# Key-tile sums moved to VectorE in six of twelve head pairs, with loads, reciprocals and key layout rearranged, in a fused attention and gated-MLP kernel

## The chip, the cores and the metric

One core of one Trainium2 chip runs the whole program. The metric is device time in microseconds (us) of one execution. Before the change three runs gave a median of 324.01 us (323.78 to 324.86).

## The reference

```python
# attention, B, H, S, D = 2, 12, 448, 64
scores = cap * np.tanh((q @ k^T) / sqrt(D) / cap)
attn = np.exp(scores - max(scores)) 
attn = attn / (sum(attn) + 1e-9)
x = (attn @ v) laid out as (B, S, H * D)
# gated MLP with a spatial gate: x is 768 wide, d_ff 1024
u, v = split(gelu(x @ w_in))
x = x + (u * (w_sg @ layernorm(v) + b_sg)) @ w_out
# second MLP: depthwise convolution of width 3 along the sequence
h = relu(x @ w2_in);  out = (h * sigmoid(conv(h))) @ w2_out
```

The inputs are scaled so that the cap is active. All of it is float32.

## The kernel before

The 24 heads are worked as 12 **pairs** N = 0 to 11, two heads in the two halves of the 128 partitions. Each pair has two half-steps, R = 2N and R = 2N + 1, in the loop at line 609, which also issues loads and calls `tick` twice per half-step; `later(k, fn)` runs `fn` k ticks on. TensorE (PE) executes one written order: `ordered` pins each product behind the one before.

- `scores` (line 386) makes the transposed scores, keys in the partitions. The even half makes key tiles 0 and 1 from split operands Q and K (12 products), the odd half tile 2 and the 64 keys that are left (8 products from raw qr and kr). Both write one PSUM tile `sc` with a single buffer, so the next half's products wait until ScalarE's tanh (line 397) has read it. ScalarE then applies exp (line 406). VectorE adds tiles 0 and 1 of the even half into `sm` (line 462).
- `values` (line 490) runs two half-steps behind: products of the exponentials with V (`V`, `vlast`), then the softmax sums as products with a tile of ones: four of `sm` after the even half, four of tile 2 and four of the rest after the odd half. Output and sums stand in PSUM `pv`.
- `norm` (line 516): ScalarE copies `pv` to `E` (line 532). For two pairs at once, POOL-issued DMAs gather the sums into `ss`; VectorE adds a guard and inverts (lines 552, 553); DMAs spread the reciprocals over DRAM `d` into `rb`; VectorE multiplies (line 569) and splits the result into X (`part`).
- `decode` turns the weights, which arrive as 64-bit floats, into split float32. One **piece** of `w_in` is a DMA into `f`, then a cast of the head (line 155 on VectorE, 153 on ScalarE), a shift-and-or (159), a cast (165) and a subtraction (168). `WIN` says at which half-step each of the 12 pieces is issued.
- After half-steps 15, 19, 23 and at the end, products of the first MLP stand among the attention's (`FILL`); from about 100 us on PE works the two MLPs.

The order of instructions on VectorE, ScalarE, POOL and SyncE's DMA queue comes from a scheduler that sorts by its own timing model, bounded by data and by `pin`, which puts an instruction behind an earlier one on its engine. These queues are strictly in order. I call the stretch from the first score product of pair N to that of pair N + 1 **window N**; PE does there scores of N and values of N - 1.

Of the kernel before, what the change touches and what calls it, by code (L numbers as in the profile page):

```python
# [16 lines left out]
ALU = mybir.AluOpType  # L17
# [20 lines left out]

TAKEN = 4

WARM = 10

K0 = 2 * P

IDLE = {0: (1, 4)}

WIN = (3, 5, 7, 9, 12, 15, 17, 19, 21, 22, 23, 24)
WOS = (0, 0, 1, 4, 4, 7, 7, 7, 10, 10, 11, 15)
W2I = (12, 12, 13, 13, 15, 17, 22, 24, 26, 30, 30, 33)
W2O = (0, 0, 1, 3, 4, 6, 7, 8, 8, 10, 10, 11, 11, 11, 11, 12, 13, 14, 15, 17, 18, 18, 19, 19)  # L50
# [3 lines left out]
def stages(  # L54
# [19 lines left out]

    now = [0]
    guards = [None]
    lasta, lastv, lastr, lasts = [None], [None], [None], [None]

    def pin(last):
        return tc.issue_after(last[0].ins) if last[0] is not None else ExitStack()  # L80
# [54 lines left out]
    heads = []  # L135
    drain = [None]

    def decode_half(hi, lo, src, pool, bufs, wait, hi_eng, top_eng, cols):

        n = src.shape[1]  # L140
        r = pool.tile([P, cols, 2], U32, tag="f64", name="f64", bufs=bufs)[:, :n]
        words = r.rearrange("p c w -> p (c w)").bitcast(U16)
        sync(words[:, : 4 * n - 1], src.rearrange("r c w -> r (c w)").bitcast(U16)[:, 1:])
        low = r[:, :, 0]
        top = words.rearrange("p (c w) -> p c w", w=4)[:, :, 2].bitcast(BF16)
        heads.append(heads.pop(0))
        hd = heads[-1][:, :n]

        def s1():
            half = hd.bitcast(F16).rearrange("p (c w) -> p c w", w=2)[:, :, 1]  # L150
            with pin(lasta), pin(lastv):
                if top_eng == "a":
                    A.activation(half, top, AF.Copy)  # L153
# [19 lines left out]
    def decode(hi, lo, src, pool, bufs, wait=(1, 2, 3), hi_eng="a", cols=512, low_eng="v", top_eng="a"):  # L173

        if heads:
            return decode_half(hi, lo, src, pool, bufs, wait, hi_eng, top_eng, cols)
        n = src.shape[1]
        r = pool.tile([P, cols, 2], U32, tag="f64", name="f64", bufs=bufs)[:, :n]
# [99 lines left out]

    def columns(pool):
        sync(gbc, g_ln.partition_broadcast(P))  # L280
        decode(cw[:, 0], cw[:, 1], conv_w, pool, *((4, (5, 6, 7)) if bounded else (3,)))

    def attention(att, psa):

# [6 lines left out]

        def load(n):
            b, p = divmod(n, NPAIR)
            qr = att.tile([P, S], F32, tag="qr", name="qr", bufs=3)
            kr = att.tile([P, S], F32, tag="kr", name="kr", bufs=3)
            k0 = 0 if n else K0
            for h in range(2):
                r = slice(h * D, (h + 1) * D)
                dma = sync if n or h else nc.scalar.dma_start
                dma(qr[r], qT[b, p, r, h])  # L300
                if k0:
                    dma(kr[r, :k0], kT[b, p, r, h, D * h : D * h + k0])

            sync(kr[:D, k0:], kT[b, p, :D, 0, k0:])
            sync(kr[D:, k0:ST], kT[b, p, D:, 1, D + k0 :])
            sync(kr[D:, ST:], kT[b, p, D:, 1, :D])
# [20 lines left out]
        def prep_k(n):  # L327
            _, kr = qraw[n]
            K = Kt[n % 2]
            lastv[0] = split(kr[:, :K0], K[:, 0], K[:, 1])  # L330

        G.dma_start(capt, cap.partition_broadcast(P))
        load(0)
# [2 lines left out]
        vlast = att.tile([P, B * NPAIR, P], F32, name="vlast")  # L336

        def load_vlast(n0, n1):
            v = vL.rearrange("b n p g c -> p (b n) g c")
            for h in range(2):  # L340
                r = slice(h * D, (h + 1) * D)
                for c in range(2):
                    sync(vlast[c * D : (c + 1) * D, n0:n1, r], v[r, n0:n1, 3, r])

        load_vlast(0, 3)
# [40 lines left out]
        def scores(N, half, then=None):  # L386
# [28 lines left out]
            for g in range(2 * half, 2 * half + 2):  # L415
# [10 lines left out]
                elif g == 2:  # L426
                    qr, kr = qraw[N]
                    x = qr.rearrange("p (i c) -> p i c", i=2)
                    for h in range(2):
                        r = slice(h * D, (h + 1) * D)  # L430
                        for i in range(2):
                            o, w = slice(i * D, (i + 1) * D), slice(K0 + i * D, K0 + (i + 1) * D)
                            ordered(ps[o, h, :2], lhsT=kr[r, w], rhs=x[r], start=True, stop=True)
                else:

                    qr, kr = qraw.pop(N)
                    for h in range(2):
                        r = slice(h * D, (h + 1) * D)
                        for i in range(2):
                            ordered(  # L440
                                ps[i * D : (i + 1) * D, h, 2], lhsT=kr[r, ST:],
                                rhs=qr[r, i * HS : (i + 1) * HS], start=True, stop=True,
                            )
                if N == 0 and g < 2:
# [45 lines left out]
        def values(N, half, done=False):  # L490
# [8 lines left out]
            ps, su, both = acc[N]  # L499
            raw = raws.pop((N, half))  # L500

            for g in range(2 * half, 3 * half + 1):
                x = raw if half else held.pop(N)
                for t in range(4):
                    h, c = divmod(t, 2)
                    ordered(
                        su[t * 32 : (t + 1) * 32],
                        lhsT=ones[2 if g < 3 else c],
                        rhs=x[:, h, g - 2 + c if g == 2 else 2] if half else x[:, h, c * HS : (c + 1) * HS],
                        start=False, stop=g == 3, tile_position=(0, t * 32), skip_group_check=True,  # L510
                    )
            if half:
# [3 lines left out]
        def norm(N, both):  # L516
# [31 lines left out]


            def s1():  # L550
                with pin(lastv):
                    V.tensor_scalar(out=ss, in0=ss, scalar1=guard, scalar2=None, op0=ALU.add)
                V.reciprocal(out=ss, in_=ss)
                ds.append(dr.tile([m, 2, 2, HS], F32, tag=f"d{m}", name="d"))
# [10 lines left out]
                        )  # L565

            def s2():
                with pin(lastv):
                    V.tensor_tensor(out=eb, in0=eb, in1=rb, op=ALU.mult)
                part(0)  # L570

            def part(i):
                with pin(lasta) if N >= 8 else pin(lastv):
                    lastv[0] = split(eb[:, i], X[:, 0, p - j + i, b], X[:, 1, p - j + i, b], "a" if N >= 8 else "v")

            k = 5 if N < 8 else 4
# [32 lines left out]
        for R in range(2 * NN + LAGS[1] + 1):  # L609
# [2 lines left out]
                columns(att)  # L612
            for j, at in enumerate(WIN):
                if at == R:
                    top_eng = "v" if R < 11 else "a"
                    wdec(*wi_piece(w_in, j // NK, j % NK), att, 4, hi_eng="v", wait=(5, 6, 7), top_eng=top_eng)
            if R < 2 * NN:
                if half == 0 and N + 2 < NN:
                    load(N + 2)
                if half == 0 and N + 1 < NN:  # L620
                    load_v(N + 1)
                if R == 6:
                    load_vlast(3, NN)
# [50 lines left out]
            tick()  # L674
        assert not due
        heads.clear()
        lasta[0] = lastv[0] = None
        lasts.clear()

    def exact_attention(att, psa):  # L680
# [420 lines left out]
```

## Time and profile before

| | |
|---|---|
| Median of 3 runs | 324.01 us |
| Profiled execution: time, span | 323.47 us, 321.3 us |
| Granted TensorE clock, mean | 0.997 |
| Busy: PE, VectorE, ScalarE, POOL | 313.5, 222.0, 206.6, 37.4 us |

The profiled execution is 0.54 us faster than the median, and 2.2 us of its time lie around the span. A matmul's record ends later than the next one starts, since they are pipelined, so durations on PE are read from start to start. Busy shares average over stages: VectorE and ScalarE are nearly idle in the last fifth.

### The profile page before, as it was taken

How to read it: one execution, taken by the hardware profiler on the slowest of the kernel's cores; microseconds unless marked ns; L12 is line 12 of the kernel's file. 1: busy time of each engine (PE TensorE's matmuls, PEld its weight loads, DVE VectorE, ACT ScalarE, POOL GpSimd, SP SyncE). 2: the span in 40 equal slices, each digit the busy share in tenths (PEclk: the TensorE clock that was granted, in tenths of full speed). 3: DMA queues.
4: the chain of work that ended last, by engine and by line, in shares of the span. 5: the costliest groups of instructions: out<-in, count | busy, mean ns of one | idle time of the engine just before them, and what ended most of it. 6: DMA issues, size and time to landing. Idle time of an engine off the chain costs nothing.

```text
span 321.3 us, 6377 instructions
## 1 busy us (share of the span) xinstructions
PE 313.5 (98%) x2398; PEld 259.3 (81%) x2398; DVE 222.0 (69%) x460; ACT 206.6 (64%) x342; POOL 37.4 (12%) x75
## 2 busy tenths in 40 slices
PE   8999999999999999999999999999999999999993
PEld 6566656666677889988999999999999999999992
DVE  3458596698568879988996899979999998000000
ACT  4999989898973447746944754568886988111010
POOL 3000141441333020211112000000000000000000
PEclk9999999999999999999999999999999999999998
DMA  3478886857242153331134670021583201110111
GB/s 114 116 219 209 246 232 151 240 165 243 93 131 89 31 159 97 93 98 50 51 98 134 203 285 1 3 65 66 141 317 98 74 27 58 58 60 29 57 57 39
DMA packets 24528, 37.73 MB, mean 117 GB/s; under 512 B 7609, under 2 KB 22473, under 8 KB 24489
## 3 DMA queue, kind: packets, MB, share of 16 engines
q1 hardware_dynamic: 22552, 34.22, 35.1%
q0 software_dynamic: 1632, 2.61, 2.8%
q8 instruction: 21, 0.34, 0.5%
q10 hardware_dynamic: 304, 0.41, 0.4%
q14 instruction: 19, 0.15, 0.2%
HBM read 34.39 MB, written 2.79 MB: 116 GB/s over the span
## 4 chain that ended last, share of the span: by engine, by line
PE 81%; DMA 2%; DVE 0%; ACT 0%; SPq 0%; issue 0%; ACTq 0%
PE mo L113 18%; PE mo L112 18%; PE mo L114 18%; PE pv L380 8%; PE sc L380 4%; PE mo L795 3%; PE mo L797 3%; PE mo L796 3%; PE mo L380 3%; PE fi L380 2%; DMA ss<-E 1%; DMA kr<-in_kT_dram 1%; PE mo L841 1%; PE mo L842 1%; DVE sm L462 0%; ACT o L982 0%
## 5 line engine op out<-in xcount | busy, mean ns | idle before, releaser
L113 PE MATMUL mo<-X,WI 128*128 128x448 f32 x120 | 43.9, 366 | 0.0
L114 PE MATMUL mo<-X,WI 128*128 128x448 f32 x120 | 43.8, 365 | 0.0
L112 PE MATMUL mo<-X,WI 128*128 128x448 f32 x120 | 43.4, 365 | 0.0
L406 ACT ACTIVATE raw<-raw 128x1344 f32<-128x1344 f32 (+2 forms) x25 | 36.4, 1460 | 0.7
L397 ACT ACTIVATE raw<-sc 128x1792 f32<-128x1792 f32 (+1 forms) x22 | 32.4, 1474 | 4.4 <-PE sc L380 4.4
L112 PE MATMUL mo<-HG,W 128*128 128x448 f32 x96 | 34.4, 365 | 0.0
L114 PE MATMUL mo<-HG,W 128*128 128x448 f32 x96 | 34.4, 365 | 0.0
L113 PE MATMUL mo<-HG,W 128*128 128x448 f32 x96 | 34.4, 365 | 0.0
L380 PE MATMUL pv<-raw,V 128*32 128x224 f32 x576 | 32.9, 357 | 0.0
L985 ACT ACTIVATE o<-mo 128x448 f32<-128x448 f32 x11 | 5.8, 540 | 34.9 <-PE mo L114 31.7
L380 PEld LDWEIGHTS pv<-raw,V 128*32 128x32 f32 x576 | 19.0, 109 | 11.5 <-issue 5.6
L113 PEld LDWEIGHTS mo<-X,WI 128*128 128x128 f32 x120 | 22.5, 188 | 1.9
L114 PEld LDWEIGHTS mo<-X,WI 128*128 128x128 f32 x120 | 22.5, 188 | 1.9
L112 PEld LDWEIGHTS mo<-X,WI 128*128 128x128 f32 x120 | 22.5, 188 | 1.9
L153 ACT ACTIVATE hs<-f 128x256 f16<-128x256 bf16 x36 | 16.6, 488 | 7.8 <-DMA f<-in_w_in_dram 4.8
L114 PEld LDWEIGHTS mo<-HG,W 128*128 128x128 f32 x96 | 18.0, 188 | 1.4
L113 PEld LDWEIGHTS mo<-HG,W 128*128 128x128 f32 x96 | 18.0, 188 | 1.4
L112 PEld LDWEIGHTS mo<-HG,W 128*128 128x128 f32 x96 | 18.0, 188 | 1.4
L168 DVE TENSOR_TENSOR WI<-f,WI 128x256 fp32r<-128x256 f32 (+1 forms) x36 | 18.2, 509 | 1.0 <-ACT WI L163 0.7
L113 PE MATMUL mo<-gl,WO 128*128 128x448 f32 x48 | 17.4, 367 | 0.0
L114 PE MATMUL mo<-GH,WO 128*128 128x448 f32 x48 | 17.2, 366 | 0.0
L380 PE MATMUL sc<-Q,K 64*128 64x448 f32 x138 | 17.2, 380 | 0.0
(156 smaller groups left out, 683.9 us busy)
## 6 DMA issues: line engine op xcount, KB each, us to landing
f<-in_w_out_dram SPq DMA_DIRECT2D x36, 255.8 KB, 2.9
f<-in_w_in_dram SPq DMA_DIRECT2D x12, 511.8 KB, 5.7
f<-in_w_in_dram SPq DMA_DIRECT2D x24, 255.8 KB, 3.4
qr<-in_qT_dram SPq DMA_DIRECT2D x23, 112.0 KB, 4.0
rb<-d POOLq DMA_DIRECT2D x22, 112.0 KB, 3.4
out_dram<-o SPq DMA_DIRECT2D x11, 224.0 KB, 2.1
V<-in_vL_dram SPq DMA_DIRECT2D x12, 192.0 KB, 4.7
kr<-in_kT_dram SPq DMA_DIRECT2D x11, 112.0 KB, 4.9
```

The lines of the kernel that those rows point to most:

```text
L112: matmul(ps, lhsT=whi, rhs=xhi, start=start, stop=False)
L113: matmul(ps, lhsT=whi, rhs=xlo, start=False, stop=False)
L114: matmul(ps, lhsT=wlo, rhs=xhi, start=False, stop=stop)
L153: A.activation(half, top, AF.Copy)
L168: V.tensor_tensor(out=lo, in0=f(low), in1=f(hi), op=ALU.subtract)
L380: lastm[0] = T.matmul(*args, **kw)
L397: lasta[0] = A.activation(x, ps, AF.Tanh, scale=sc)
L406: lasta[0] = A.activation(x, x, AF.Exp, scale=creg)
L795: T.matmul(ps, lhsT=xs(0, k), rhs=WI[1][:, 0, k], start=k == 0, stop=False)
L796: T.matmul(ps, lhsT=xs(0, k), rhs=WI[1][:, 1, k], start=False, stop=False)
L797: T.matmul(ps, lhsT=xs(1, k), rhs=WI[1][:, 0, k], start=False, stop=k == NK - 1)
L985: A.activation(o, ps, AF.Copy, scale=0.5)
```

## The change

It has five parts. (1) In pairs 1, 2, 3, 5, 7 and 9 (`ADD`) VectorE adds tile 2 into `sm` after the odd half's exp; the four products of `sm` with ones move from the even to the odd half of `values`, and the four of tile 2 go. (2) `w_in` pieces are issued up to three half-steps sooner with the same half-step of decoding for pieces 0 to 7 (`WIN`, `WAIT`), in three buffers in place of four; the convolution weights get a tile of their own. (3) q and k of a pair are loaded a pair sooner, in four buffers; kr is 512 wide, and from pair 1 on each head takes one k load of 448 columns, where the second head took two. `vlast` comes in four groups of three pairs. (4) The reciprocal of a group of pairs starts two ticks later for N < 8. (5) Decoding, guard addition, multiplication and the second `part` are pinned behind the new addition or a newer `sm`.

```diff
+ADD = (1, 2, 3, 5, 7, 9)
-WIN = (3, 5, 7, 9, 12, 15, 17, 19, 21, 22, 23, 24)
+WIN = (1, 3, 5, 7, 10, 13, 15, 17, 20, 22, 23, 24)
+WAIT = (9, 9, 9, 9, 9, 9, 9, 9, 7, 5, 5, 5)
+LAST = {0: (0, 3), 4: (3, 6), 8: (6, 9), 12: (9, 12)}
...
@@ decode_half
-            with pin(lasta), pin(lastv):
+            with pin(lasta), pin(lastv), pin(lastx):
...
@@ columns
-        decode(cw[:, 0], cw[:, 1], conv_w, pool, *((4, (5, 6, 7)) if bounded else (3,)))
+        how = dict(bufs=1, wait=(5, 6, 7), cols=3 * NF, tag="c64") if bounded else dict(bufs=3)
+        decode(cw[:, 0], cw[:, 1], conv_w, pool, **how)
...
@@ load
-            qr = att.tile([P, S], F32, tag="qr", name="qr", bufs=3)
-            kr = att.tile([P, S], F32, tag="kr", name="kr", bufs=3)
+            qr = att.tile([P, S], F32, tag="qr", name="qr", bufs=4)
+            kr = att.tile([P, 4 * P], F32, tag="kr", name="kr", bufs=4)
...
+            if n:
+                for h in range(2):
+                    r, o = slice(h * D, (h + 1) * D), D * (1 - h)
+                    sync(kr[r, o : o + S], kT[b, p, r, h])
...
@@ scores
             if half:
                 soft(raw, ps)
+                if N in ADD:
+                    x = held[N].rearrange("p h (i c) -> p h i c", i=2)
+                    lastx[0] = V.tensor_tensor(out=x, in0=x, in1=raw[:, :, :2], op=ALU.add)
...
@@ values
-            for g in range(2 * half, 3 * half + 1):
-                x = raw if half else held.pop(N)
+            for g in ((0, 3) if half else ()) if N in ADD else ((2, 3) if half else (0,)):
+                x = raw if g else held.pop(N)
...
@@ norm
             def s1():
-                with pin(lastv):
+                with pin(lastv), pin(lastx):
...
             def s2():
-                with pin(lastv):
+                with pin(lastv), pin(lastx):
...
             def part(i):
-                with pin(lasta) if N >= 8 else pin(lastv):
+                own = pin(sms[max(sms)]) if i and N < 8 else ExitStack()
+                with pin(lasta) if N >= 8 else pin(lastv), own:
...
-            k = 5 if N < 8 else 4
+            k = 7 if N < 8 else 4
...
@@ loop over R
-                    top_eng = "v" if R < 11 else "a"
-                    wdec(*wi_piece(w_in, j // NK, j % NK), att, 4, hi_eng="v", wait=(5, 6, 7), top_eng=top_eng)
+                    k, top_eng = WAIT[j], "v" if j < 4 else "a"
+                    wdec(
+                        *wi_piece(w_in, j // NK, j % NK), att, 3, hi_eng="v", wait=(k, k + 1, k + 2), top_eng=top_eng
+                    )
             if R < 2 * NN:
-                if half == 0 and N + 2 < NN:
-                    load(N + 2)
+                for n in ((2,), (3,))[R] if R < 2 else range(N + 3, min(N + 4, NN)) if half == 0 else ():
+                    load(n)
...
-                if R == 6:
-                    load_vlast(3, NN)
+                if R and R in LAST:
+                    load_vlast(*LAST[R])
```

On PE, window 3 (scores of pair 3, values of pair 2) reads so before:

```order
L380 MATMUL sc<-Q,K_88 128x448 x12
L380 MATMUL pv<-raw,V 32x224 x16
L380 MATMUL pv<-sm,ones_144 32x224 x4
L380 MATMUL sc<-qr,kr 64x2x224 x4
L380 MATMUL sc<-qr,kr 64x224 x4
L380 MATMUL pv<-raw,vlast 64x224 x4
L380 MATMUL pv<-raw,V 32x224 x8
L380 MATMUL pv<-raw,ones_144 32x224 x4
L380 MATMUL pv<-raw,ones_142 32x224
L380 MATMUL pv<-raw,ones_143 32x224
```

and so with the change:

```order
L391 MATMUL sc<-Q,K_88 128x448 x12
L391 MATMUL pv<-raw,V 32x224 x16
L391 MATMUL sc<-qr,kr 64x2x224 x4
L391 MATMUL sc<-qr,kr 64x224 x4
L391 MATMUL pv<-raw,vlast 64x224 x4
L391 MATMUL pv<-raw,V 32x224 x8
L391 MATMUL pv<-sm,ones_143 32x224 x4
L391 MATMUL pv<-raw,ones_141 32x224
L391 MATMUL pv<-raw,ones_142 32x224
```

The four products of `sm` stand half a window later, in the place of the four of tile 2. Windows 2, 4, 6, 8 and 10 change in the same way; the others read as before, and ScalarE's order in the attention is the same throughout.

On VectorE, around the addition of pair 4 (the last row here; `f_453` is the third piece, `ss` the sums of pairs 0 and 1), before:

```order
L462 TENSOR_TENSOR sm<-raw 128x896
L106 CAST Q<-qr 128x448
L106 CAST K_88<-kr 128x256
L109 TENSOR_TENSOR Q<-qr,Q 128x448
L109 TENSOR_TENSOR K_88<-kr,K_88 128x256
L552 TENSOR_SCALAR ss<-ss,one 128x14
L155 CAST hd_135<-f_453 128x512
L553 RECIPROCAL ss<-ss 128x14
L159 SCALAR_TENSOR_TENSOR f_453<-f_453,hd_135 128x512
L165 CAST WI_76<-f_453 128x512
L168 TENSOR_TENSOR WI_76<-f_453,WI_76 128x512
L462 TENSOR_TENSOR sm<-raw 128x896
```

and with the change, from the new addition of pair 3 to the addition of pair 4 (`f_281` and `f_361` are the second and third piece):

```order
L471 TENSOR_TENSOR sm<-sm,raw 128x896
L161 CAST hd_135<-f_281 128x512
L566 TENSOR_SCALAR ss<-ss,one 128x14
L161 CAST hd_134<-f_361 128x512
L165 SCALAR_TENSOR_TENSOR f_281<-f_281,hd_135 128x512
L567 RECIPROCAL ss<-ss 128x14
L165 SCALAR_TENSOR_TENSOR f_361<-f_361,hd_134 128x512
L171 CAST WI_76<-f_281 128x512
L171 CAST WI_76<-f_361 128x512
L174 TENSOR_TENSOR WI_76<-f_281,WI_76 128x512
L174 TENSOR_TENSOR WI_76<-f_361,WI_76 128x512
L476 TENSOR_TENSOR sm<-raw 128x896
```

Two pieces now stand between the new addition of pair 3 and the addition of pair 4, where one stood; the Q and K of a pair are split one pair sooner, ahead of all this.

On VectorE ahead of the addition of pair 6 (the last row), with the change (`rb` holds the reciprocals of pairs 0 and 1, `ss` the sums of pairs 2 and 3):

```order
L471 TENSOR_TENSOR sm<-sm,raw 128x896
L161 CAST hd_135<-f_450 128x512
L583 TENSOR_TENSOR E<-E,rb 128x896
L165 SCALAR_TENSOR_TENSOR f_450<-f_450,hd_135 128x512
L112 CAST X<-E 128x448
L171 CAST WI_76<-f_450 128x512
L115 TENSOR_TENSOR X<-E,X 128x448
L566 TENSOR_SCALAR ss<-ss,one 128x14
L174 TENSOR_TENSOR WI_76<-f_450,WI_76 128x512
L567 RECIPROCAL ss<-ss 128x14
L476 TENSOR_TENSOR sm<-raw 128x896
```

Before, `ss` of pairs 2 and 3 stood ahead of the multiplication by `rb`, and the fourth piece was done a pair sooner.

## Rows read from the trace of the kernel before

**Rows 1.** Windows 2, 3, 5, 7, 8: length, PE, PEld, DVE, ACT, POOL busy, clock, DMA.
```profile
17.71:24.53 6.82, 6.82 (x109) 4.39 (x109) 2.90 (x6) 6.76 (x6) 0.67 (x1) 1.00 0.69 210
24.53:31.37 6.84, 6.84 (x113) 4.40 (x109) 5.46 (x11) 6.62 (x6) 0.62 (x1) 1.00 0.92 222
...
38.22:45.78 7.56, 7.04 (x113) 4.19 (x110) 6.62 (x13) 6.58 (x6) 2.42 (x4) 1.00 0.86 255
...
52.61:61.35 8.74, 8.45 (x119) 5.26 (x115) 8.06 (x17) 8.48 (x8) 3.95 (x7) 1.00 0.79 208
61.35:68.18 6.83, 6.83 (x110) 4.37 (x109) 4.23 (x10) 5.23 (x4) 1.31 (x3) 1.00 0.57 149
```
**Rows 2.** Timeline of PE in window 3: start us, us, instruction, [idle before <-releaser].
```profile
24.53 1.49 PE L380 MATMUL sc<-Q,K 64*128 64x448 f32 x12
25.96 1.76 PE L380 MATMUL pv<-raw,V 128*32 128x224 f32 x32
27.50 0.60 PE L380 MATMUL pv<-sm,ones 128*32 128x224 f32 x8
28.03 1.36 PE L380 MATMUL sc<-qr,kr 64*64 64x448 f32 x16
...
30.48 0.96 PE L380 MATMUL pv<-raw,ones 128*32 128x224 f32 x16
```
**Rows 3.** Timeline of PE in windows 5 and 7, where VectorE's sum comes last.
```profile
39.64 1.76 PE L380 MATMUL pv<-raw,V 128*32 128x224 f32 x32
41.92 0.59 PE L380 MATMUL pv<-sm,ones 128*32 128x224 f32 x8 [0.52 <-DVE sm L462]
...
54.03 1.76 PE L380 MATMUL pv<-raw,V 128*32 128x224 f32 x32
56.08 0.58 PE L380 MATMUL pv<-sm,ones 128*32 128x224 f32 x8 [0.29 <-DVE sm L462]
```
**Rows 4.** Timeline of ScalarE in windows 2 and 3: tanh of pair 2, copy, tanh of pair 3.
```profile
19.36 1.67 ACT L397 ACTIVATE raw<-sc 128x1792 f32<-128x1792 f32 x1
...
25.20 0.71 ACT L532 ACTIVATE E<-pv 128x672 f32<-128x672 f32 x1
26.06 1.66 ACT L397 ACTIVATE raw<-sc 128x1792 f32<-128x1792 f32 x1 [0.16 <-PE sc L380]
```
**Rows 5.** Timeline of ScalarE in window 8: tanh of pair 8, cast of a piece, tanh of pair 9.
```profile
62.89 1.66 ACT L397 ACTIVATE raw<-sc 128x1792 f32<-128x1792 f32 x1 [1.56 <-PE sc L380]
...
69.44 0.79 ACT L153 ACTIVATE hd<-f 128x512 f16<-128x512 bf16 x1
70.08 1.65 ACT L397 ACTIVATE raw<-sc 128x1792 f32<-128x1792 f32 x1
```
**Rows 6.** Timeline of VectorE: third piece, fourth piece up to pair 5's addition, sums of pairs 2 and 3.
```profile
38.44 0.47 DVE L155 CAST hd<-f 128x512 f16<-128x512 bf16 x1 [3.83 <-DMA f<-in_w_in_dram]
...
43.82 0.47 DVE L155 CAST hd<-f 128x512 f16<-128x512 bf16 x1 [0.58 <-DMA f<-in_w_in_dram]
...
46.44 1.08 DVE L462 TENSOR_TENSOR sm<-raw 128x896 f32<-128x896 f32 x1
...
51.70 0.23 DVE L552 TENSOR_SCALAR ss<-ss,one 128x14 f32<-128x14 f32 x1 [2.80 <-DMA ss<-E]
```
**Rows 7.** Timeline of ScalarE and POOL: exp of pair 3's odd half, reciprocals' DMAs of pairs 0 and 1.
```profile
30.78 1.33 ACT L406 ACTIVATE raw<-raw 128x1344 f32<-128x1344 f32 x1
...
39.32 0.59 POOL L556 DMA_DIRECT2D d<-ss  x1 [12.50 <-DVE ss L553]
...
44.57 2.36 POOL L562 DMA_DIRECT2D rb<-d  x4 [4.04 <-DMA d<-ss]
```
**Rows 8.** DMA issues by line: count, KB each, median us from issue to landing.
```profile
f<-in_w_in_dram SPq DMA_DIRECT2D x12, 511.8 KB, 5.7
...
rb<-d POOLq DMA_DIRECT2D x22, 112.0 KB, 3.4
```
**Rows 9.** The long stretch after the attention: length and busy, columns as in rows 1.
```profile
85.00:316.00 231.00, 230.97 (x1250) 206.57 (x1250) 166.94 (x346) 130.37 (x278) 17.53 (x28) 1.00 0.29 93
```

More of the change, by code (lines that the diff above doesn't have):

```diff
@@ L76, in stages @@
     guards = [None]
-    lasta, lastv, lastr, lasts = [None], [None], [None], [None]
+    lasta, lastv, lastx, lasts = [None], [None], [None], [None]
     def pin(last):
@@ L136, in stages, with decode_half @@
     drain = [None]
-    def decode_half(hi, lo, src, pool, bufs, wait, hi_eng, top_eng, cols):
+    def decode_half(hi, lo, src, pool, bufs, wait, hi_eng, top_eng, cols, tag):
         n = src.shape[1]
-        r = pool.tile([P, cols, 2], U32, tag="f64", name="f64", bufs=bufs)[:, :n]
+        r = pool.tile([P, cols, 2], U32, tag=tag, name="f64", bufs=bufs)[:, :n]
         words = r.rearrange("p c w -> p (c w)").bitcast(U16)
@@ L171, in decode_half, with decode @@
             later(k, fn)
-    def decode(hi, lo, src, pool, bufs, wait=(1, 2, 3), hi_eng="a", cols=512, low_eng="v", top_eng="a"):
+    def decode(hi, lo, src, pool, bufs, wait=(1, 2, 3), hi_eng="a", cols=512, low_eng="v", top_eng="a", tag="f64"):
         if heads:
-            return decode_half(hi, lo, src, pool, bufs, wait, hi_eng, top_eng, cols)
+            return decode_half(hi, lo, src, pool, bufs, wait, hi_eng, top_eng, cols, tag)
         n = src.shape[1]
-        r = pool.tile([P, cols, 2], U32, tag="f64", name="f64", bufs=bufs)[:, :n]
+        r = pool.tile([P, cols, 2], U32, tag=tag, name="f64", bufs=bufs)[:, :n]
         sync(r, src)
@@ L293, in load @@
             b, p = divmod(n, NPAIR)
-            qr = att.tile([P, S], F32, tag="qr", name="qr", bufs=3)
-            kr = att.tile([P, S], F32, tag="kr", name="kr", bufs=3)
-            k0 = 0 if n else K0
+            qr = att.tile([P, S], F32, tag="qr", name="qr", bufs=4)
+            kr = att.tile([P, 4 * P], F32, tag="kr", name="kr", bufs=4)
+            k0 = K0
             for h in range(2):
@@ L300, in load @@
                 dma(qr[r], qT[b, p, r, h])
[L301 to L306, printed above, removed]
+                if n == 0:
+                    dma(kr[r, D : D + k0], kT[b, p, r, h, D * h : D * h + k0])
+            if n:
+                for h in range(2):
+                    r, o = slice(h * D, (h + 1) * D), D * (1 - h)
+                    sync(kr[r, o : o + S], kT[b, p, r, h])
+            else:
+                sync(kr[:D, D + k0 :], kT[b, p, :D, 0, k0:])
+                sync(kr[D:, D + k0 : S], kT[b, p, D:, 1, D + k0 :])
+                sync(kr[D:, :D], kT[b, p, D:, 1, :D])
             qraw[n] = qr, kr
@@ L329, in prep_k @@
             K = Kt[n % 2]
-            lastv[0] = split(kr[:, :K0], K[:, 0], K[:, 1])
+            lastv[0] = split(kr[:, D : D + K0], K[:, 0], K[:, 1])
         G.dma_start(capt, cap.partition_broadcast(P))
@@ L338, in load_vlast @@
         def load_vlast(n0, n1):
[L339 to L345, printed above, removed]
+            v = vL.rearrange("b n (h d) g c -> h d (b n) g c", h=2)
+            for c in range(2):
+                for h in range(2):
+                    r = slice(h * D, (h + 1) * D)
+                    sync(vlast[c * D : (c + 1) * D, n0:n1, r], v[h, :, n0:n1, 3, r])
+        load_vlast(*LAST[0])
         if WARM:
@@ L431, in scores @@
                         for i in range(2):
-                            o, w = slice(i * D, (i + 1) * D), slice(K0 + i * D, K0 + (i + 1) * D)
+                            o, w = slice(i * D, (i + 1) * D), slice(D + K0 + i * D, D + K0 + (i + 1) * D)
                             ordered(ps[o, h, :2], lhsT=kr[r, w], rhs=x[r], start=True, stop=True)
@@ L437, in scores @@
                     for h in range(2):
-                        r = slice(h * D, (h + 1) * D)
+                        r, w = slice(h * D, (h + 1) * D), slice(S * (1 - h), S * (1 - h) + D)
                         for i in range(2):
                             ordered(
-                                ps[i * D : (i + 1) * D, h, 2], lhsT=kr[r, ST:],
+                                ps[i * D : (i + 1) * D, h, 2], lhsT=kr[r, w],
                                 rhs=qr[r, i * HS : (i + 1) * HS], start=True, stop=True,
@@ L508, in values @@
                         lhsT=ones[2 if g < 3 else c],
-                        rhs=x[:, h, g - 2 + c if g == 2 else 2] if half else x[:, h, c * HS : (c + 1) * HS],
+                        rhs=x[:, h, c if g == 2 else 2] if g else x[:, h, c * HS : (c + 1) * HS],
                         start=False, stop=g == 3, tile_position=(0, t * 32), skip_group_check=True,
@@ L676, in attention @@
         heads.clear()
-        lasta[0] = lastv[0] = None
+        lasta[0] = lastv[0] = lastx[0] = None
         lasts.clear()
```

## The prediction

> **What bounds the kernel now.** I read the stretches of the pairs first, then PE's timeline in one of them, then who PE waits for, then ScalarE's timeline, and last the long stretch behind.
>
> The attention costs about 6.83 us per window where nothing is filled in, and PE is busy in all of it [rows 1]. Two windows are longer for no work: window 5 lasts 7.56, 0.73 more, and window 7 has 0.29 of PE idle inside its 8.74. From 85 to 316 us PE is busy 230.97 of 231.00 us [rows 9]. So whatever PE gets done sooner before 85 us moves the end by as much, and what is saved on other engines moves nothing by itself.
>
> PE is not alone, though. In window 3 its score products end, and 0.1 us later ScalarE starts the tanh at 26.06, after only 0.16 us of idle; before that it ran from 19.36 to 25.91 (25.20 + 0.71) with no idle entry [rows 4]. ScalarE has 6.62 us of work in 6.84 [rows 1]. In window 8 it has none to spare: from the tanh of pair 8 at 62.89 to that of pair 9 at 70.08 are 7.19 us, a piece's cast among them, and no idle entry stands at 69.44 or 70.08 [rows 5]. The reader should see two engines that take turns, with PE 0.2 us ahead of ScalarE in the plain windows and behind it in those with a cast.
>
> **The removed products.** Four products of `sm` take 27.50 to 28.03 [rows 2], 0.53 us; the eight of tile 2 and the rest take 30.48 to 31.37, the window's end [rows 1, 2], so four of them 0.45. Six sets at 0.45 to 0.53 make 2.7 to 3.2 us if nothing else binds. I take 0.53 at the place of the `sm` products, because half a window later four products of `sm` stand where the four of tile 2 stood, at the same price.
>
> Something else binds. With the `sm` products gone from the even half, the V products of window 3 end at 27.50 and the odd half's scores are next. They write the one `sc` buffer, which the tanh reads until 26.06 + 1.66 = 27.72 [rows 2, 4]. They start at about 27.75 in place of 28.03: **0.28 us** is kept of the 0.53. ScalarE can follow: it has 0.16 idle, and a successor that waits for nothing starts before the instruction ahead has ended (69.44 + 0.79 = 70.23 against 70.08, 0.15) [rows 4, 5], together 0.31. If that overlap does not come, 0.16 is kept, which is the lower bound for these windows.
>
> - Window 2: the tanh starts at 19.36 because ScalarE was busy (no idle entry) and ends at 21.03. The odd half's products stood 3.50 us into the window (28.03 - 24.53), that is at 21.21. Kept: 0.15.
> - Windows 3, 4, 6: 0.28 each, 0.84.
> - Windows 8 and 10: ScalarE's 7.19 us from tanh to tanh stay, and the next odd half waits for that tanh. Kept: nothing. I checked one of the two; the other has the same order.
>
> Sum of the products: **1.0 us**, from 0.6 (0.15 x 4) to 3.2 (no bound by ScalarE).
>
> **The two stalls.** In window 5 the V products take 1.54 us elsewhere (25.96 to 27.50), yet the `sm` products follow after 2.28 (39.64 to 41.92): 0.74 lost. In window 7, 54.03 to 56.08 is 2.05: 0.51 lost [rows 2, 3]. Together **1.25 us**, both ended by VectorE's `sm`. Behind the first is a piece's cast that waited 3.83 us for its DMA, behind the second the guard addition that waited 2.80 us for the gathered sums [rows 6]; the sum that PE needs stood in order behind them.
>
> Does the change end both, and what is late next? The third piece's DMA goes out two half-steps, one window of 6.84, sooner: landing by 38.44 - 6.84 = 31.6. The addition of pair 3 can start when its exp ends, 30.78 + 1.33 = 32.1, less the 0.4 that the windows 2 and 3 have saved: 31.7. It takes 1.08, the two pieces behind it 2.62 each (43.82 to 46.44), the guard addition and reciprocal 0.4 [rows 6, 7]. The sum of pair 4 then starts at 38.4 and is done at 39.5. PE wants it at 41.18 (39.64 + 1.54), less 0.7 saved: 40.5. **Margin 1.0 us.** At window 7 the guard addition comes half a window, 3.4 us, later than before, more than the 2.80 it waited, and no longer ahead of the multiplication. Ahead of the sum of pair 6 stand the new addition of pair 5 (from about 45.1), a piece of 2.62, a multiplication by `rb` (as wide as the additions, 1.1), a split of half as much in two instructions (1.0, an estimate from that) and 0.4 for the reciprocals: done at 45.1 + 1.08 + 5.1 + 1.08 = 52.4. PE wants it at 54.03 + 1.54 - 1.7 = 53.9. Margin 1.5. So I take both stalls as gone; the bounds are 0 and 1.25, since VectorE may lose its margins.
>
> **The rest of the change.** Six additions of 1.08 us put 6.5 us on VectorE. Windows 3, 5 and 7 have it busy 5.46 of 6.84, 6.62 of 7.56 and 8.06 of 8.74, window 2 only 2.90 [rows 1]. It fits, and if it did not, the `sm` would be late again as above. The first addition is wanted only at the end of window 2. The wide k load drops one issue in each of 11 pairs on SyncE's queue, and `vlast` adds eight; neither is waited for by PE, and loads a pair sooner hide both. If that cover went, Q and K would be late for a window, up to the 5.7 us of a piece's landing [rows 8] that now stands ahead of pair 3's load. Three buffers in place of four: the convolution weights no longer take one, so the last two pieces reuse the same pieces' buffers as before; the others are issued sooner than needed. The tail after 85 us keeps its order and shifts as a whole [rows 9]. All of these: 0.
>
> **Sum.** 1.0 + 1.25 = 2.25, rounded 2.2 us. The profiled execution took 323.47 and would take 321.3; the median of the runs shown is 0.54 above it, so from 324.01 I forecast **321.8 us**.
>
> **Rivals.**
>
> - *ScalarE never binds* (7%). The 0.53 is kept six times: 3.2 + 1.25 = 4.4, 319.6 us. Against it stand the missing idle entries of window 8 [rows 5] and the tanh that holds `sc` [rows 4].
> - *Only one half of it comes* (20%): the stalls go but ScalarE keeps its pace (0.15 x 4), or the products pay and one stall stays because VectorE is fuller. 1.25 + 0.6 = 1.85 at best, 1.0 at worst: 322.2 to 323.0.
> - *Nothing comes of it* (14%). VectorE has 6.5 us more in order, and each new addition waits for an exp with pieces and reciprocals queued behind it. If the margins of 1.0 and 1.5 are used up by late DMAs, PE stalls as long as before, and what the products save is given back: 324.0 us, or a little under. It takes a third piece that lands 2.5 us later than reckoned (34.2; its cast's turn is about 33.2). For it: DMA engines are busy 0.92 of window 3 [rows 1]. Against: the piece is issued a window sooner.
> - *Slower through `rb`* (4%). The multiplication by `rb` of pairs 0 and 1 now stands ahead of the sum of pair 6. The reciprocal comes at about 35; POOL's chain took 39.32 to 44.57, 5.25, to the first issue of `rb` and 2.36 for four issues [rows 7], and landing takes 3.4 [rows 8]: 46.0, just before its turn at 46.7. With the margin of 1.5, PE stalls when it lands after 48.2, and the total is slower than 324.98 once it lands after 51.4. If each of the four issues had to sit out a piece of VectorE (2.62), they would take 10.5 in place of 2.36: landing at 54.1, 5.9 lost, 327.7 us. Against it: the four issues ran at 0.59 each while VectorE did the fourth piece, 43.82 to 46.44 [rows 6, 7].
>
> The Trainium skill, SBUF — State Buffer, section "SBUF: two separate sides", speaks for this last rival: a DMA issued from GpSimd needs its descriptors written through a port that VectorE's two-port copies lock, and one is said to go from about 620 ns to about 3100 ns. By that the four issues would take some 12.4 us and the estimate would be near 330 us; this trace disagrees, with 0.59 us per issue beside VectorE's casts [rows 6, 7].
>
> **How the numbers follow.** The forecast has 55%, and its own range is 321.2 to 322.3. About 0.3%, 1.0 us, is what a measurement here can tell from no change, so faster means under 323.04 and slower over 324.98. Faster: 55, 7 and most of the 20, less some doubt that all cases share: 0.76. Same: the 14 and the rest of the 20: 0.18. Slower: 0.06. The range leaves out the slow end, the case of ScalarE never binding and half of the case of nothing: **320.7 to 324.0**.
>
> **What would show it.** The PE timeline should have no wait for `sm` in windows 5 and 7; windows 3, 4 and 6 should last about 6.55, window 5 about 6.8, window 7 about 8.25, and windows 8 and 9 together as long as before, less 0.1 at most. PE should show small waits for ScalarE's tanh before the odd scores in windows 2, 3, 4, 6, 8 and 10, which were not there. On VectorE the 3.83 and 2.80 us waits should be gone. The forecast is wrong if VectorE's sum of pair 4 or 6 ends after its margin, if windows with an addition keep 6.83, or if window 8 shrinks by over 0.2.

## The result and the profile after

| | before | changed |
|---|---|---|
| median of 22 runs, us | 324.47 (323.31 to 325.96) | 327.01 (324.54 to 330.93) |
| ratio changed to before, 95% interval | | 1.0065 [1.0046, 1.0084] |
| span of the profiled execution, us | 321.3 | 323.6 |

The changed kernel is 0.65% slower, about 2.1 us; I had forecast 2.2 us faster. Its runs also lie 6.4 us apart, those of before 2.7. The ratios leave out runs that the comparison counts as disturbed (5 of the 22 here; below, 5 of 12 for e2, 4 of 12 for e3, one each for e1 and e4) and the medians do not, so the two need not agree.

The windows come first: windows 3, 5, 7, 8 and 9 of the changed kernel, columns as in [rows 1].

```profile
24.51:31.20 6.69, 6.61 (x104) 4.40 (x101) 6.37 (x14) 6.44 (x6) 0.63 (x1) 1.00 0.68 179
...
37.89:44.76 6.87, 6.87 (x113) 4.41 (x110) 3.77 (x9) 6.65 (x6) 2.76 (x5) 1.00 0.68 176
...
51.46:59.74 8.28, 8.28 (x118) 5.44 (x114) 7.95 (x19) 8.09 (x8) 3.43 (x6) 1.00 0.69 175
59.74:66.34 6.60, 6.52 (x101) 4.05 (x100) 1.85 (x3) 5.43 (x5) 0.63 (x1) 1.00 1.05 256
66.34:75.68 9.34, 8.53 (x119) 5.28 (x115) 8.70 (x17) 8.68 (x9) 3.51 (x6) 1.00 0.47 132
```

Windows 5 and 7 have lost their stalls (7.56 to 6.87, 8.74 to 8.28), and window 3 is 0.15 shorter. Pair 8 starts at 59.74, 1.61 us sooner than before. Then it turns: window 9 takes 9.34, where it took 8.46 before:

```profile
68.18:76.64 8.46, 8.43 (x120) 5.78 (x116) 7.04 (x15) 8.40 (x9) 2.66 (x5) 1.00 0.72 224
```

PE's timeline of the changed kernel shows that place and one more, behind the attention:

```profile
70.41 0.59 PE L391 MATMUL pv<-sm,ones 128*32 128x224 f32 x8 [0.75 <-DVE sm L476]
...
98.83 3.92 PE L391 MATMUL mo<-X,WI 128*128 128x448 f32 x18
105.34 0.98 PE L391 MATMUL pv<-E,sel 128*64 128x224 f32 x8 [2.59 <-DVE E L606]
106.25 3.94 PE L391 MATMUL fi<-X,WI 128*128 128x448 f32 x18
```

Before, the first of the fill products above (`mo`, x18) and the products that spread the reciprocals of pair 11 (`pv<-E,sel`) followed each other without a wait:

```profile
99.88 3.93 PE L380 MATMUL mo<-X,WI 128*128 128x448 f32 x18
103.73 0.98 PE L380 MATMUL pv<-E,sel 128*64 128x224 f32 x8
```

At 98.83 the changed kernel is still 1.05 us ahead; at 105.34 it is 1.61 behind. Its last product ends 1.6 us later than before, and the rest of the 2.3 us of span is the last store. Both waits name VectorE, so I read its timeline:

```profile
66.81 1.09 DVE L583 TENSOR_TENSOR E<-E,rb 128x896 f32<-128x896 f32 x1 [5.18 <-DMA rb<-d]
...
69.32 1.03 DVE L476 TENSOR_TENSOR sm<-raw 128x896 f32<-128x896 f32 x1
...
92.95 0.23 DVE L566 TENSOR_SCALAR ss<-ss,one 128x14 f32<-128x14 f32 x1 [6.55 <-DMA ss<-E]
...
102.94 0.23 DVE L566 TENSOR_SCALAR ss<-ss,one 128x7 f32<-128x7 f32 x1 [1.80 <-DMA ss<-E]
...
103.32 0.29 DVE L605 TENSOR_SCALAR E<-E,one 128x224 f32<-128x224 f32 x1
103.64 1.55 DVE L606 RECIPROCAL E<-E 128x224 f32<-128x224 f32 x1
```

VectorE stands 5.18 us at the multiplication by `rb` of pairs 2 and 3 with the sum of pair 8 behind it. It stands 6.55 us for the gathered sums `ss` of pairs 8 and 9, and 1.80 us for those of pair 10, with the reciprocal of pair 11 (L605, L606), which PE wants, in order behind. What makes these transfers late shows on POOL (GpSimd), which issues them all, in order:

```profile
82.12 0.58 POOL L570 DMA_DIRECT2D d<-ss  x1 [5.58 <-DVE ss L567]
88.08 2.10 POOL L576 DMA_DIRECT2D rb<-d  x4 [5.38 <-DMA d<-ss]
90.17 0.66 POOL L548 DMA_DIRECT2D ss<-E  x1
93.75 0.56 POOL L570 DMA_DIRECT2D d<-ss  x1 [2.92 <-DVE ss L567]
95.75 2.09 POOL L576 DMA_DIRECT2D rb<-d  x4 [1.44 <-DMA d<-ss]
97.82 0.75 POOL L548 DMA_DIRECT2D ss<-E  x1
```

The same stretch of the kernel before:

```profile
77.82 0.55 POOL L556 DMA_DIRECT2D d<-ss  x1 [6.98 <-DVE X L106]
...
82.73 2.10 POOL L562 DMA_DIRECT2D rb<-d  x4 [3.72 <-DMA d<-ss]
85.11 0.68 POOL L534 DMA_DIRECT2D ss<-E  x1 [0.29 <-ACT E L532]
```

In both kernels a gather (`ss<-E`) stands behind the four issues of `rb`, and these wait for `d` to land. Before, `d` of pairs 6 and 7 went out at 77.82, so the queue was free when the sums came: the gather waited for ScalarE's eviction alone (0.29). In the changed kernel the reciprocals are due one half-step later and `d` goes out at 82.12; the gather then sits behind `rb` until 90.17, 5.1 us later than before. The chain of the changed kernel that ended last runs through just these transfers (start us, us, what):

```profile
58.12 8.57 DMA rb<-d
...
82.12 5.67 DMA d<-ss
...
90.17 2.66 DMA ss<-E
...
97.82 5.02 DMA ss<-E
103.64 1.56 DVE E L606
```

DMA has 8% of that chain, where it has 2% of the chain of before.

### The profile page after: what moved, and what is told of

The parts are those of the page before. It is cut to its first block, busy times and chain, and to the rows that moved or that the text cites. A ratio compares the mean times of both kernels' runs of the same rounds, so it can differ in the third digit from the quotient of the medians.

```text
span 323.6 us, 6282 instructions
## 1 busy us (share of the span) xinstructions
PE 312.0 (96%) x2350; PEld 258.9 (80%) x2350; DVE 225.1 (70%) x466; ACT 206.1 (64%) x342; POOL 37.8 (12%) x75
## 4 chain that ended last, share of the span: by engine, by line
PE 80%; DMA 8%; ACT 4%; DVE 3%; POOL 2%; issue 1%; DVEq 0%; ACTq 0%
PE mo L119 18%; PE mo L118 18%; PE mo L120 18%; PE pv L391 7%; PE sc L391 7%; PE mo L814 3%; PE mo L812 3%; PE mo L813 3%; ACT raw L408 3%; DMA rb<-d 3%; DMA ss<-E 2%; DMA d<-ss 2%; POOL rb L576 2%; PE wps L364 1%; PE fi L391 1%
## 5 line engine op out<-in xcount | busy, mean ns | idle before, releaser
L391 PE MATMUL sc<-qr,kr 64*64 64x448 f32 (+1 forms) x192 | 17.0, 454 | 1.0 <-ACT raw L408 0.6
```

Of the source, the lines that this page charges most:

```text
L391: lastm[0] = T.matmul(*args, **kw)
```

## Experiments

Three theories stood at first. **A**: a serial chain of late reciprocals, transfers and VectorE. **B**: the sooner loads crowd the transfers. **C**: the six additions fill VectorE. The diffs are against the changed kernel unless said otherwise; "the end wait" is PE's wait before the spread products in the profiled execution. "Ratio to before" is to runs of the kernel before that were made beside it, with a 95% interval.

### One part undone at a time

Reciprocals back (`e1_recip_back`):

```diff
-            k = 7 if N < 8 else 4
+            k = 5 if N < 8 else 4
```

> The changed kernel with one number undone: the reciprocals of a pair of pairs are due 5 ticks behind it again, not 7, so that each stands ahead of the multiplication by rb of the pairs before, not behind it. Everything else of the change stays. Theory A (serial chain: late reciprocal, late d, late rb, the next reciprocal behind that rb's multiplication, and so on to the last reciprocals): VectorE's wait of 5.18 us for rb at 66.8 us falls below 2 us, its wait of 6.55 us for ss at 93 falls by over half, PE's 2.59 us before the spread products and its 0.75 us in window 9 go, and the time is 322 to 324.5 us. Theory B (transfers crowded by the sooner loads): rb still takes about 8 us from issue to landing and the waits move, so 325.5 to 327.5. Theory C (VectorE is too full by the six additions): 325.5 to 327.5 as well, with the sums late.

Without additions (`e2_no_add`):

```diff
-ADD = (1, 2, 3, 5, 7, 9)
+ADD = ()
```

> The changed kernel without the six additions on VectorE, so with all sets of products with ones back on TensorE; loads, wide keys and later reciprocals stay. Theory A (serial chain of reciprocals): the stalls near 70 and 103 us stay and the products cost their 0.5 to 1.0 us again: 327 to 328.5 us. Theory B (crowded transfers): the same 327 to 328.5, as no transfer changes. Theory C (additions fill VectorE): the stalls go and the time is 322.5 to 324.5.

Old loads (`e3_old_loads`; the pieces have four buffers again, q and k three each, and the convolution weights go back to the pieces' tag; `vlast` stays in four groups):

```diff
-WIN = (1, 3, 5, 7, 10, 13, 15, 17, 20, 22, 23, 24)
-WAIT = (9, 9, 9, 9, 9, 9, 9, 9, 7, 5, 5, 5)
+WIN = (3, 5, 7, 9, 12, 15, 17, 19, 21, 22, 23, 24)
+WAIT = (5, 5, 5, 5, 5, 5, 5, 5, 5, 5, 5, 5)
...
-                for n in ((2,), (3,))[R] if R < 2 else range(N + 3, min(N + 4, NN)) if half == 0 else ():
+                for n in range(N + 2, min(N + 3, NN)) if half == 0 else ():
```

> The changed kernel with the old times of the loads: Q and K two pairs ahead in three buffers each, the pieces of the first weights at the old half-steps with the old waits and four buffers, the convolution weights in one of those. Additions, wide keys and later reciprocals stay. Theory B (crowded transfers): the DMA share from 46 to 67 us falls from 0.74 to 1.05 to about 0.7, rb lands within 4.5 us of its issue, VectorE's wait of 5.18 us for rb goes, and the time is 321.5 to 324. Theory A (serial chain of reciprocals): some wait for rb or ss over 3 us stays on VectorE, PE's wait before the spread products stays above 1 us, 325 to 327.5. Theory C (additions): 325 to 328, with sums later than in the changed kernel since the pieces land later.

The kernel before with the reciprocals late (`e4_before_recip_late`, against the kernel before):

```diff
-            k = 5 if N < 8 else 4
+            k = 7 if N < 8 else 4
```

> The kernel before with one number of the change: reciprocals due 7 ticks behind their pairs in place of 5. Theory A (serial chain): the stall of window 7 (0.51 us) may go, but VectorE waits for rb or ss of later pairs and PE waits over 1 us before the spread products or in a window behind 60 us: 1 to 2.5 us slower than before, ratio 1.003 to 1.008. Theories B and C (crowded transfers, additions): 0 to 0.5 us faster than before, ratio 0.998 to 1.000.

| | median (range), us | ratio to before | end wait, us |
|---|---|---|---|
| e1 | 324.55 (322.14 to 327.32) | 0.9992 [0.9965, 1.0019] | 1.67 |
| e2 | 324.49 (322.39 to 332.16) | 0.9953 [0.9916, 0.9989] | 0.6 |
| e3 | 324.85 (321.88 to 330.08) | 0.9970 [0.9930, 1.0011] | none |
| e4 | 325.42 (323.66 to 328.76) | 1.0035 [1.0004, 1.0065] | none |

No theory has all four right. The last is A's: one late number makes the kernel before slower by 0.35%, and its VectorE and PE (window 9) show the stall, with no addition and no load moved:

```profile
67.30 1.09 DVE L569 TENSOR_TENSOR E<-E,rb 128x896 f32<-128x896 f32 x1 [7.06 <-DMA rb<-d]
...
71.19 1.09 DVE L462 TENSOR_TENSOR sm<-raw 128x896 f32<-128x896 f32 x1
```

```profile
72.33 0.59 PE L380 MATMUL pv<-sm,ones 128*32 128x224 f32 x8 [1.75 <-DVE sm L462]
```

e4 has no end wait, though, so late reciprocals alone make the stall in window 9 and not the one at the end. And A said that e1 loses the end wait: VectorE's wait for `rb` is gone and the one for the sums of pairs 8 and 9 falls from 6.55 to 3.61, but 1.67 of the end wait stayed, and PE waits 0.61 for the sum of pair 6 and 0.32 in window 11. A said that e2 and e3 stay slow, and each of them wins back about half of the runs: 7 of 12 of e2 took 322.4 to 325.1 and 5 took 327.3 to 332.2, and 6 of 12 of e3 took 321.9 to 323.7 and 6 took 326.0 to 330.1. I read this as a chain that arrives in time more often, not always, with an emptier VectorE or the old loads. That is not shown, since the profiles kept of e2 and e3 are of quick runs (323.29 and 322.83). What stayed in e1 stands in the chain that ended last there:

```profile
87.77 4.69 DMA ss<-E
...
97.45 5.04 DMA ss<-E
```

With the reciprocals at their old place, the gathers of pairs 9 and 10 still went out behind `rb` and took 4.7 and 5.0 us to land. What joined the reciprocals to the end was still open.

### The end of the chain, and both ends

The changed kernel ran again as a control (`c1_changed_again`), and with the last reciprocals, those of pair 10, pinned behind those of pair 11 (`f1_last_recip_behind`):

```diff
-                with pin(lastv), pin(lastx):
+                with pin(lastv), pin(lastx), pin(drain) if last else ExitStack():
                     V.tensor_scalar(out=ss, in0=ss, scalar1=guard, scalar2=None, op0=ALU.add)
```

> The changed kernel itself, so that the kernels of this call stand beside it on one chip. All theories: 325 to 328 us, ratio to before 1.003 to 1.010, PE's wait before the spread products over 1 us.

> The changed kernel with one pin more: the guard addition and reciprocal of pair 10 stand behind those of pair 11 in VectorE's order, so that the latter no longer waits behind the gathered sums of pair 10. Nothing else moves. If the loss behind 85 us is this order (the sums of pair 10 landing late ahead of what PE wants), the 2.59 us before the spread products go and the time falls by 2 to 2.6 us: 323.5 to 325.5. If late transfers or the additions set the end otherwise, the wait only changes its place: 326 to 328.

`f2_recip_back_and_behind` is this pin with e1's edit, and `f3_old_loads_recip_behind` the pin with those of e1 and e3:

> The changed kernel with reciprocals due after 5 ticks again and the pin of the run before. Theory A (serial chain): neither the chain nor its end reaches PE; PE has less than 0.5 us of waits for VectorE and the time is 321.3 to 322.8, ratio to before 0.990 to 0.995. Theory B (crowded transfers by the sooner loads): sums stay late somewhere by over 0.5 us, 322.8 to 325.

> As the run before, but with the old times and buffers of the loads, so that additions and wide keys are all that is left of the change, with the pin. Theory A: the pieces land later than in the run before, so VectorE may be late with the sums of pair 4 or 6, 322 to 324 us. Theory B: 321 to 322.5, better than the run before by 0.5 us or more.

| | median (range), us | ratio to before | end wait, us |
|---|---|---|---|
| c1 | 328.63 (325.95 to 330.40) | 1.0139 [1.0098, 1.0179] | 4.57 |
| f1 | 324.48 (323.13 to 327.32) | 1.0035 [1.0006, 1.0065] | 0.99 |
| f2 | 322.84 (321.68 to 323.95) | 0.9969 [0.9951, 0.9986] | none |
| f3 | 322.47 (321.92 to 323.31) | 0.9965 [0.9950, 0.9980] | none |

c1 is slower than any theory had it. The order at the end is worth 4.1 us of the median (328.63 to 324.48; 3.4 by the ratios), more than I expected; the 0.99 that stays in f1 follows ScalarE's eviction of pair 11, which VectorE waits 0.85 for. f1 is still slower than before, and its runs spread; which of the other waits varies there, I did not see. With the reciprocals back as well, both kernels beat the one before, and the spread of the runs shrinks to 2.3 and 1.4 us. f2 and f3 differ in the loads and agree within their intervals, so the sooner loads cost nothing measurable in time once the end has room. B is not wholly out, however: f2's PE still waits 0.75 us for the sum of pair 6, where A said under 0.5 us and B over 0.5, and its 322.84 lies at the edge between the two. f3 has no such wait. What falls is B as the whole cause.

The order alone would not explain 4.1 us from a wait of 2.59. The profiled execution of c1 does. PE:

```profile
106.97 1.76 PE L391 MATMUL pv<-E,sel 128*64 128x224 f32 x8 [4.57 <-DVE E L606]
108.67 5.65 PE L391 MATMUL fi<-X,WI 128*128 128x448 f32 x18
```

and the stretches around it (columns as in [rows 1], the granted clock third from the end):

```profile
104.00:106.00 2.00, 0.00 (x0) 0.00 (x0) 1.36 (x4) 0.00 (x0) 0.55 (x1) 0.90 0.00 0
106.00:108.00 2.00, 1.02 (x6) 0.84 (x8) 1.93 (x4) 0.00 (x0) 0.66 (x2) 0.50 0.02 2
...
110.00:112.00 2.00, 2.00 (x7) 1.79 (x6) 1.92 (x6) 1.02 (x3) 0.00 (x0) 0.50 0.29 60
112.00:114.00 2.00, 2.00 (x11) 1.83 (x10) 0.91 (x3) 0.00 (x0) 0.00 (x0) 0.89 0.18 64
```

While PE waits, the granted clock falls from 1.00 to 0.50, the lower of its two levels (1.2 of 2.4 GHz), and it comes back between 112 and 114 us. The spread products take 1.76 in place of 0.98 and the fill products 5.65 in place of 3.94, so a wait of 4.57 costs 7.1 (4.57 + 0.78 + 1.71). In the first profile of the changed kernel, with 2.59, the clock stayed at 1.00:

```profile
104.00:106.00 2.00, 0.66 (x8) 0.57 (x8) 1.97 (x3) 0.00 (x0) 0.55 (x2) 1.00 0.02 2
```

Three profiles of this one kernel show end waits of 2.59, 4.57 and (below) 3.10: the chain arrives at another time in each, and in two of the three the clock added to the bill. I take that for the spread of its runs, without a profile of each. The mean granted clock, which every run has, points the same way: it was 0.994 to 0.999 in the six quickest of the 22 runs and 0.984 to 0.993 in the six longest.

### Additions or loads alone, and more additions

`g4_loads_alone` is e2's and e1's edit together, and `g3_two_more_adds` is f3 with `ADD = (1, 2, 3, 4, 5, 6, 7, 9)`, beside f3 again.

> Of the change only the loads and the wide keys are left: no additions, reciprocals due after 5 ticks. Theory A (the reciprocals' place is what costs): the sooner pieces end the stall of window 5 (0.74 us) and nothing else is lost: 323 to 324 us, ratio 0.996 to 1.000, PE's wait before the spread products under 1.7 us as with reciprocals back alone. Theory B (sooner loads crowd the transfers): PE waits over 1 us for VectorE somewhere behind 60 us, ratio above 1.001.

> The kernel with old loads, reciprocals back and the pin behind pair 11, with additions for pairs 4 and 6 too, so that eight sets of products go. Each of the windows 4 to 6 that gains an addition should shrink by 0.15 us as windows 3, 4 and 6 did, from 6.86 to about 6.70 and 8.27 to 8.1: 0.3 us faster than the same kernel with six, beside it in this call, if VectorE has room; if an addition makes a sum late, PE waits for it and it is 0 to 1 us slower.

> The kernel with old loads, reciprocals back and the pin behind pair 11, once more, as the one to compare the one with eight additions with: ratio to before 0.995 to 0.998.

| | median (range), us | ratio to before | end wait, us |
|---|---|---|---|
| g4 | 323.34 (322.30 to 325.47) | 0.9972 [0.9948, 0.9997] | none |
| g3 | 322.84 (321.76 to 324.08) | 0.9939 [0.9919, 0.9960] | none |
| f3 again | 322.72 (321.80 to 323.49) | 0.9936 [0.9913, 0.9958] | none |

The loads and wide keys alone do no harm and gain 0.28%, as A said; B had them slower. The profiled execution of g4 (324.56) has one wait of PE, 1.23 us for ScalarE at 185 us in the MLP, which the others do not have; I leave it open. Two more additions gain nothing: window 5 comes out as expected (45.00 - 38.31 = 6.69, 6.86 in f3), but window 7 takes 60.24 - 51.69 = 8.55 in place of 8.27, with 0.23 us of PE waiting for the new sum. VectorE is busy in all 8.55 us of that window (7.34 of 8.27 in f3), so there it has no room left.

### GpSimd's queue as a link

What was left of A was the way from the late reciprocals to the late gathers. `h1_gathers_on_sync` changes only who issues the gathers; VectorE's order differs from the changed kernel's by one row. The changed kernel ran beside it (`c2_changed_third`), and f3 with the same edit (`h2_best_gathers_on_sync`).

```diff
-                G.dma_start(ss[j * P // m : (j + 1) * P // m], e[::32, u : u + HS])
+                nc.sync.dma_start(ss[j * P // m : (j + 1) * P // m], e[::32, u : u + HS])
```

> The changed kernel with only the gathers of the sums (ss) issued by SyncE, no longer by GpSimd, where they stand behind the four issues of rb, which wait for d. If that queue is a link of the chain, the gathers go out when their sums are evicted, VectorE's wait of 6.55 us for ss and PE's wait before the spread products go or fall below 1 us, and the time falls by 2 us or more against the changed kernel in this call: 323 to 325.5. If the late reciprocals alone make the chain, or crowded transfers, the wait before the spread products stays above 1.5 us and the time within 1 us of the changed kernel.

> The changed kernel itself, beside the run before on the same chip: 325 to 329 us.

> The kernel with old loads, reciprocals back and the pin behind pair 11, with the gathers issued by SyncE as well. It has no wait of PE for VectorE left, so if only such waits are to be had, 0 to 0.3 us from that kernel: ratio to before 0.993 to 0.998. If the gathers' issues hold up loads on SyncE, K or Q come late and it is slower than 0.998.

| | median (range), us | ratio to before | end wait, us |
|---|---|---|---|
| h1 | 322.59 (321.90 to 323.44) | 0.9960 [0.9942, 0.9978] | none |
| c2 | 328.16 (326.60 to 328.50) | 1.0114 [1.0088, 1.0140] | 3.10 |
| h2 | 323.12 (321.96 to 325.41) | 0.9988 [0.9964, 1.0012] | none |

This shows the queue as the link. With later reciprocals, additions and sooner loads all in place, taking the gathers off GpSimd's queue makes the changed kernel 5.6 us faster (328.16 to 322.59; 5.0 by the ratios) and 0.4% faster than the one before. SyncE's issues in h1:

```profile
84.25 0.54 SPq L548 DMA_DIRECT2D ss<-E  x1
...
90.14 0.55 SPq L548 DMA_DIRECT2D ss<-E  x1
```

and VectorE's reciprocals in h1:

```profile
87.70 0.23 DVE L566 TENSOR_SCALAR ss<-ss,one 128x14 f32<-128x14 f32 x1 [1.76 <-DMA ss<-E]
...
99.11 0.22 DVE L566 TENSOR_SCALAR ss<-ss,one 128x7 f32<-128x7 f32 x1
...
100.04 0.34 DVE L605 TENSOR_SCALAR E<-E,one 128x224 f32<-128x224 f32 x1 [0.47 <-ACT E L603]
```

The gathers of pairs 9 and 10 go out at 84.25 and 90.14, 5.9 and 7.7 us sooner than on POOL (90.17, 97.82). It is the place in the queue that helps, and not a quicker transfer: VectorE has the sums of pair 9 at 87.70, 3.4 us behind the issue, where the gather on POOL landed after 2.66. Of the wait of 6.55 us, 1.76 stays. VectorE reaches pair 11's guard addition at 100.04, not 103.32. In f3, which has room already, the same edit gains nothing and may cost (h2 has 0.9988, f3 had 0.9965 and 0.9936); h2's profile has a wait of 0.57 us for the sum of pair 6. Five versions beat the kernel before, by 0.3 to 0.6% and with intervals that stay under 1: f3, g3, h1, f2 and g4. e2, whose runs reach 332 us, I don't count.

## Why the prediction was wrong

**The removed products: right in kind, 0.70 in place of 1.0 us.** f3's PE waits for nothing but 0.2 us of ScalarE, so its windows measure the term without the stalls. Windows 2, 3 and 9 to 10 of f3:

```profile
18.20:25.02 6.82, 6.61 (x102) 4.40 (x101) 4.13 (x9) 6.76 (x6) 0.67 (x1) 1.00 0.68 187
25.02:31.70 6.68, 6.65 (x104) 4.42 (x101) 5.76 (x11) 6.49 (x6) 0.74 (x1) 1.00 0.89 254
...
66.88:75.39 8.51, 8.46 (x120) 5.82 (x116) 6.55 (x13) 8.45 (x9) 2.75 (x5) 1.00 0.73 204
75.39:82.09 6.70, 6.62 (x102) 4.39 (x102) 5.78 (x12) 5.75 (x5) 1.20 (x2) 1.00 0.66 202
```

Window 2 kept nothing (I said 0.15), windows 3, 4 and 6 kept 0.16, 0.16 and 0.15 (0.28 each), windows 8 and 9 together 0.10 and window 10 0.13 (nothing). The wait for the tanh is where I put it; in the changed kernel's window 3 the odd scores started 3.25 us into the window, against 3.50. But behind that wait the odd half took 3.44 us in place of 3.34, as this timeline of PE shows. From start to start the score group took 1.18 as before; the 0.10 comes with the `vlast` products behind it, 0.59 (28.94 to 29.53), where they took 0.49 before (29.21 to 29.70).

```profile
27.76 1.46 PE L391 MATMUL sc<-qr,kr 64*64 64x448 f32 x16
28.94 0.66 PE L391 MATMUL pv<-raw,vlast 64*64 64x224 f32 x8
29.53 0.98 PE L391 MATMUL pv<-raw,V 128*32 128x224 f32 x16
```

Window 8 of the changed kernel shrank by 0.23, which I had named as a sign against me. ScalarE's tanh to tanh there was 7.10 (61.28 to 68.38), no faster to speak of, and of the 0.15 that f3 gains in window 8 it gives 0.05 back in window 9. So ScalarE binds there over the two windows, but less tightly than I argued: 0.10 and 0.13 were kept where I had nothing.

**The two stalls: right, 1.17 of 1.25 us.** In f3 window 5 fell from 7.56 to 6.86 and window 7 from 8.74 to 8.27. The changed kernel's sum of pair 6 ended later than I worked out, 53.89 (52.86 + 1.03) against 52.4, just at the 53.9 at which PE wants it; a wait of 1.99 us for `rb` stood ahead of it. PE came to it at 54.45 and did not wait. Products and stalls together gave 1.87 us in f3 (65.76 - 63.89 from pair 2 to pair 11), where I had 2.25.

**The step that failed** is "The tail after 85 us keeps its order and shifts as a whole [rows 9]. All of these: 0", and with it the reciprocals' new place, which I priced only by the 2.80 us wait that it takes away. I followed VectorE's queue past the moved step, but not POOL's: the later reciprocal issues `d` later, POOL issues `rb` only when `d` has landed, and the next gather stands behind. Each link is a few us ([rows 7] had `rb` 5.25 us behind `d`). They add up because the gather's landing releases the next reciprocal. One row of the kernel before held the margin: POOL's gather at 85.11 waited 0.29 for ScalarE, so there was next to none. The 3.4 us by which I let the guard additions slide was longer than that margin.

A second term of the same sum was put at 0 on a wrong reading: "Three buffers in place of four", with "the others are issued sooner than needed". `WIN` moves no piece by more than two half-steps (the text ahead of the prediction says three), and the tenth piece not at all. With three buffers SyncE waits 5.9 us for VectorE to be done with the one that the tenth piece needs. That piece goes out at 81.74, where it went at about 75.5, and `gbc` (256 KB) stands behind it in SyncE's queue. Before:

```profile
75.96 0.42 SPq L86 DMA_DIRECT2D gbc<-in_g_ln_dram  x1
```

and with the change, at the very start of the slow `d`:

```profile
82.12 0.43 SPq L92 DMA_DIRECT2D gbc<-in_g_ln_dram  x1
```

What such loads may do to the chain's transfers can be seen in f2 and f3, which issue the gather of pair 9 at 84.12 and 84.23: it took 6.7 us to land in f2 (three buffers, `gbc` at 82.05) and 2.5 in f3 (four buffers, `gbc` at 75.81). No run changes the buffers alone, and none has the additions with old loads and old reciprocals but no pin, so what this adds to the loss stays open.

**The rivals.** The one through `rb`, at 4%, had the right machinery, the wrong pair and the wrong price. Its 3.7 us of loss (327.7) came nearest to the measured 2.1, which was luck. The four issues took 2.10 and 2.09 us in the changed kernel, as before, so nothing of theirs was stretched, and the Trainium skill's rule in SBUF — State Buffer, section "SBUF: two separate sides", does not show in these rows either. What was long is the transfer: `rb` of pairs 2 and 3 took 8.57 us on the chain and `d` of pairs 6 and 7 5.67, where the same `d<-ss` released `rb` 2.0 us behind its issue at 93.75. SyncE had issued a 512 KB piece at 81.74 and the 256 KB of `gbc` at 82.12, beside that `d`. The Trainium skill, DMA: Bandwidth & Descriptors, section "Issuing engines are not separate DMA queues", says that transfers of all issuing engines run on the same 16 DMA engines and interleave; these rows agree, though no run here took `gbc` away. "Nothing comes of it" had the wrong place: it looked for the loss in the sums of windows 5 and 7, which were in time.

## What to carry to other kernels

When a step moves, follow every queue that its issues pass through to the next instruction that waits in it, and see how long that one waited before: a wait of 0.29 us for its own data means that a delay of 3 us arrives in full. A DMA that depends on nothing late should not be issued behind one that waits for another transfer; here moving eleven 3.5 KB gathers to another queue was worth 5.6 us, and nothing in f3, where the chain had room already. And where PE waits for a chain of transfers, the spread of the runs tells more than the median.

## What the runs showed of the chip

I had not expected a small wait to be paid for twice. During waits of 4.57 us (c1) and 3.10 us (c2) the granted clock fell to 0.50 and stayed there for some 7 us, and the products in it cost 2.5 to 2.7 us more; with 2.59 us it stayed at 1.00. In c2:

```profile
104.87 1.76 PE L391 MATMUL pv<-E,sel 128*64 128x224 f32 x8 [3.10 <-DVE E L606]
106.56 5.83 PE L391 MATMUL fi<-X,WI 128*128 128x448 f32 x18
```

Nor had I expected a write of 7 KB to DRAM to vary so much: from the issue of `d` to the first issue of `rb` took 2.0 us at 93.75 and 6.0 us at 82.12 in one execution.
